# Input chunks ahead of weights, decode steps moved into the mixed stage, splits moved one step forward: one change to a retention-and-two-MLP kernel

## The chip, the cores and the metric

One core of one Trainium2 chip runs the kernel. The time is the device time of one execution in microseconds, the median of three runs: 1015.4 us before the change (1014.79 to 1015.66).

## The reference

Four batches, 8 heads, 768 positions, 64 dimensions per head; everything is float32 on the chip, and the weights come as float64.

```
state = gamma_h * state + k_t (x) v_t ;  y_t = q_t . state / 8      # retention, H=8, S=768
x = y as 3072 tokens x 512
h = (x @ w1) * (x @ w2) @ w3 ;  x = h @ w_out                       # 512 -> 1024 -> 1024 -> 512
h = x @ w_in ;  g = h * sigmoid(1.702 h) ;  out = g @ w_out2        # 512 -> 2048 -> 512
```

## The kernel before, in words

Every product runs on TensorE (PE) as three single-pass matmuls, hi·hi, hi·lo and lo·hi (`mm3`, L231 to L234), so each operand is split: ScalarE (ACT) writes the rounded high part (`split`, L247) and VectorE (DVE) the rest (`residue`, L160).

**Weights.** They arrive as pairs of 32-bit words, 36 tiles of two 512 KB halves ("raw"), fetched through SyncE's (SP's) DMA queue by `fetch` (L107) into `R_BUFS` = 5 buffers. `weight_steps` (L169) turns one tile into floats in eight to ten steps: ACT takes a scaled magnitude (`magnitude`, L126), VectorE clamps, shifts, ors in the low word and the sign; GpSimd (POOL) forms the seven operand blocks of tiles 12 and up (`seven`, L162) and stores them to DRAM. `work(n)` runs n steps: where the code calls it decides where the decode stands on ACT, VectorE and POOL.

**Order.** It is written by hand (`manual_schedule`); each engine runs its instructions in program order, and so does each of the two issuing queues, SP's and POOL's: what stands behind an instruction that waits, waits too.

**Stages.**
1. Attention: 24 chunks of 128 positions, six per batch. `load(c)` (L313, POOL's queue) brings q, k, v of a chunk (128x2048, 1 MB) into one of four buffers; `scores`, `masked`, `updates`, `outputs` work on it; `fill(c, at)` after each of the four runs decode steps and, from c = 6 on, a gate product. The decay factors `dy` of chunk places 1 to 5 are made on POOL (L306) from `cy`, a DMA on SP's queue.
2. Gates: for six blocks of 512 tokens (`ORDER`, n = 0 to 5; n = 0 lies in the attention) and eight tiles t each, `gate_mm` makes 12 matmuls of x·w1 and 12 of x·w2 into two `psm` banks (six buffers) and `gate_out` multiplies them (ACT copy L270, DVE L271); `gate_first` (n < 3) stores pairs from two `h` buffers by SP (L284), `gate_second` builds five sums `g` on VectorE and POOL (L981, L982) and stores them by POOL's queue (L983). The x operand of the next block is reloaded and split beside it (`split_x`). Between the last gates of n = 1 and the first of n = 2 stand the eight rows of w3·w_out (`mix_mm`, 24 matmuls and `work(7)` each). In n = 5 `opening(t)` loads and splits what the next stage starts with.
3. Blend: 21 products (seven per pair of token blocks, each 24 matmuls of 512 columns into two `m` banks) of `h` with the mixed weights. Product n needs `l` loaded by SP (L759, four buffers), its high part by ACT and its low part by VectorE. After each product `ahead` runs four decode steps as long as there are any, and later prepares the next stage.
4. Expand (w_in, sigmoid gate) in four slices of eight quads. `fetch_left` (L503) brings the operand blocks `op<-sp` of 896 KB.
5. Contract (w_out), not touched.

Of the kernel before, what the change touches and what calls it, by code (L numbers as in the profile page):

```python
# [7 lines left out]
F32 = mybir.dt.float32  # L8
# [8 lines left out]
P = 128  # L17
NT = B * S
NCK = S // P
NC = B * NCK  # L20
NP = H // 2
TB = 512
# [20 lines left out]
def tile_kernel(  # L43
# [60 lines left out]
    fetched = used = 0  # L104
    allowed = R_BUFS

    def fetch():  # L107

        nonlocal fetched
        if fetched >= min(used + allowed, 2 * len(tiles)):  # L110
            return
        i, c = divmod(fetched, 2)
        fetched += 1
        src = tiles[i][0][:, c * WC : (c + 1) * WC].bitcast(I32)
        raw = prep.tile([P, WC, 2], I32, tag="r", bufs=R_BUFS, name="raw")
        nc.sync.dma_start(raw, src.rearrange("p (c w) -> p c w", w=2))
        raws.setdefault(i, []).append(raw)

# [40 lines left out]
    def residue(hi, lo, x):  # L159
        nc.vector.tensor_tensor(lo, x, hi.bitcast(F32), ALU.subtract)  # L160

    def seven(i, a1, a2):  # L162
        st = homes["st"].tile([P, 1024], F32, tag="st", bufs=2, name="st")
        four(st, a1, a2)
        store_parts(i, a1, a2, st)

# [121 lines left out]
    class Attention:  # L288
# [122 lines left out]
        def run(self, fill):  # L411

            self.scores(0)
            self.masked(0)
            for c in range(NC):
                if c + 1 < NC:
                    self.scores(c + 1)
                fill(c, 0)
                if c + 1 < NC:
                    self.masked(c + 1)  # L420
                fill(c, 1)
                self.updates(c)
                self.next_state(c)
                if c + 3 < NC:
                    self.load(c + 3)
                if c + 2 in range(2, NCK):
                    self.factors(c + 2)
                fill(c, 2)
                self.outputs(c)
                fill(c, 3)  # L430


# [68 lines left out]
    def fetch_left(n, queue=nc.gpsimd):  # L501
        t = left[n][:, 1].rearrange("p b c -> p (b c)")
        queue.dma_start(t.bitcast(F32), sp[n])  # L503
# [8 lines left out]
    class Expand:  # L512
# [75 lines left out]
        def run(self):  # L588
            self.open = nxt = None
            for n in range(1, NQ):  # L590
                left_tile(n)
                if n < NQ - 1:
                    fetch_left(n)
            self.results = [self.result(j) for j in range(2)]
            split_left(1)
            for s in range(NS):

                for j in range(NQ):

                    def step(at):  # L600
                        nonlocal nxt
                        more = s + 1 < NS
                        if more and (j, at) == (2, 3):
                            nxt = operands(s + 1, self.py)
                            next(nxt)
                        elif more and (j, at) in NEXT:
                            next(nxt)
                        elif s and (j, at) in ((0, 0), (0, 1)):
                            next(nxt)
                        if not more and (j, at) in OPENING:  # L610
                            for run in OPENING[j, at]:
                                run()

                    self.quad(s, j, step)
            for _ in self.fourth():
                pass
# [147 lines left out]
    def split_h(n, a, b, hi):  # L764
        for c, d, t in lo2[n]:
            c0, d0 = max(a, c), min(b, d)
            if c0 < d0:
                lo = t[:, c0 - c : d0 - c]
                split(hi[:, c0 - a : d0 - a], lo, lo.bitcast(F32))
# [3 lines left out]
    def split_wm(n):  # L773
        hi, lo = wm[blends[n][1]]
        split(hi, lo, lo.bitcast(F32))

    def opening(t):
        if t:
            name = blends[t - 1][1]
            wm[name] = wtile("wg")  # L780
            nc.sync.dma_start(
                wm[name][1].bitcast(F32), sm[PART[name]].rearrange("p k c -> p (k c)")
            )
        if t == 1:
            x = spare.tile([P, 7, TB], F32R, tag="ope", name="h0")
            hi2[0] = x[:, NM:]
            load_h(0, 0, NM, x[:, :NM])
        if t == KF - 2:
            for k in (0, 2):
                load_h(1, k, k + 2, prep.tile([P, 2, TB], F32R, tag="r", bufs=R_BUFS, name="h1"))  # L790
        if t in (4, 5, 6):
            split_h(0, t - 4, t - 3, hi2[0][:, t - 4 : t - 3])
        if t in (6, 7):
            split_wm(t - 6)

    def blend(p, ps, todo):
        ws = {
# [19 lines left out]
            nc.gpsimd.dma_start(yd[i][:, e], t)  # L817

        load_turn(2)
        hi2[1], k3 = tile("h", 2), tile("h", 2)[:, 0]  # L820
        load_turn(3)
        held = [p.tile([P, TB], F32, tag="o", bufs=2, name="c")]
        ready = [value()]
        split_h(0, 3, 4, k3.rearrange("p (a t) -> p a t", a=1))
        for n, (i, name) in enumerate(blends):
# [47 lines left out]
    with tc.manual_schedule():  # L873
# [4 lines left out]
        with (  # L878
            tc.tile_pool(name="p0", bufs=1, reuse_waits="tile") as p0,
            tc.tile_pool(name="ps0", bufs=1, space=PSUM, reuse_waits="tile") as ps0,  # L880
        ):
            attention = Attention(p0, ps0)
            nc.sync.dma_start(attention.dv, cv)
            nc.sync.dma_start(attention.mask, cmask)
            fetch()
            attention.load(0)
            fetch()
            attention.load(1)
            nc.sync.dma_start(attention.step[:, :NCK], cstep)
            attention.factors(0)  # L890
            attention.load(2)
            attention.factors(1)
            for n in range(2, R_BUFS):
                fetch()
            gates = 0
            late = []

            def wide():
                return ps0.tile([P, TB], F32, tag="w", bufs=2, name="psg")

            def first_gate():
                nonlocal gates
                late.append((gates, 0, gate_mm(gates, 0, wide)))
                gates += 1

            def fill(c, at):
                work(1)
                while late:
                    gate_first(*late.pop())
                if c in range(13, 21) and at == 1:  # L910
                    d = (c - 13) % 4
                    if c < 17:
                        reload(ORDER[1], d)
                    else:
                        split_x(ORDER[1], d)
                if at == 3 and c >= CPB and gates < min(complete, KF):
                    first_gate()

            work(3)
            attention.run(fill)  # L920
            while gates < KF:
                weight(gates)
                first_gate()
                work(4)
                gate_first(*late.pop())
        with (
# [43 lines left out]
            def gate_second(t, i, ab):  # L970
                nonlocal b12, g
                b = hb[0]
                if t % 2 == 0:
                    b12 = pb.tile([P, TB], F32, tag="b", bufs=2, name="b12")
                    g = pb.tile([P, 5, TB], F32, tag="g", bufs=2, name="g")
                    gate_out(b12, ab)
                    nc.vector.tensor_tensor(g[:, 1], b12, b[:, 0], ALU.subtract)
                    return
                gate_out(g[:, 0], ab)
                nc.vector.tensor_tensor(g[:, 3], g[:, 0], b12, ALU.subtract)  # L980
                nc.gpsimd.tensor_tensor(g[:, 2], g[:, 0], g[:, 1], ALU.subtract)  # L981
                nc.gpsimd.tensor_tensor(g[:, 4], b[:, 1], g[:, 2], ALU.subtract)  # L982
                nc.gpsimd.dma_start(hd[i // 2][:, t // 2, 2:], g)  # L983
                hb.pop(0)

            g = None
            b12 = None
            for n, i in list(enumerate(ORDER))[1:]:
                nxt = ORDER[n + 1] if n + 1 < NB else None
                for t in range(KF):  # L990
# [11 lines left out]
                        split_x(nxt, t - KD)  # L1002
                    if n >= 4 and t > 2:
                        allowed = R_BUFS - 2
                    work((1 if nxt is None else 3) if n > 2 else 8)
                    (gate_second if n > 2 else gate_first)(t, i, ab)
                    while rows < KF and (complete > W3 + rows or (n, t) == (2, KF - 1)):
                        ps = mix_mm(rows)
                        work(7)
                        mix_out(rows, ps)  # L1010
                        rows += 1
                        if rows == KF:
                            stage.close()
                            pb = homes["st"] = stage.enter_context(
                                tc.tile_pool(name="b2", bufs=1, reuse_waits="tile")
                            )
        inner.close()
        homes["st"] = second.enter_context(
            tc.tile_pool(name="wa", bufs=1, side="right", reuse_waits="tile")
# [135 lines left out]
```

## Time and profile before

| | |
|---|---|
| median of the runs | 1015.4 us |
| the profiled execution, its span | 1016.0 us, 1014.2 us |
| PE busy in the span | 971.7 us (96%) |
| VectorE, ScalarE, GpSimd busy | 727.0 (72%), 448.8 (44%), 209.8 us (21%) |
| mean granted TensorE clock | 0.984 of 2.4 GHz |
| DMA | 265 GB/s over the span |

The span runs from the first to the last instruction of the core, the execution's time has 1.8 us more around it. PE is the engine that carries the work, so the time can be read as its busy time plus its gaps. Matmul records have the ends modelled; the clock is a share of full speed, and a stretch at 0.50 runs its matmuls at half pace.

### The profile page before, as it was taken

The page shows a single profiled execution, that of the slowest core. Times are in us where ns is not written, and L with a number is a line of the kernel's source. Part 1 is how long each engine was busy: PE and PEld are TensorE (multiplying, and loading weights), DVE is VectorE, ACT ScalarE, POOL GpSimd, SP SyncE. Part 2 cuts the span into 40 slices and gives each one's busy share as a digit, 9 for nine tenths or more (in the row PEclk, how much of TensorE's full clock was granted, in tenths as well). Part 3 has the DMA queues.
Part 4 walks back from the last instruction along what each step waited for, and adds up shares of the span by engine and source line. Part 5 has one row for each costly group of instructions (what it writes and reads, how often), then busy time and mean ns, then how long its engine had stood idle before and what let it go on. Part 6 is the DMA issues. An engine that isn't in the chain of part 4 may idle for free.

```text
span 1014.2 us, 14850 instructions
## 1 busy us (share of the span) xinstructions
PE 971.7 (96%) x5608; PEld 841.1 (83%) x5608; DVE 727.0 (72%) x954; ACT 448.8 (44%) x793; POOL 209.8 (21%) x254
## 2 busy tenths in 40 slices
PE   4999999999989999899997999999999999999998
PEld 3788778888868888678886999999999888888886
DVE  4767768889998975874883796776868555657662
ACT  4666554442323211455453755454546443445330
POOL 3101000248876764430322000000000000000000
PEclk9899999999989999999997999999999999999999
DMA  8789956569999977998846745546497978767871
GB/s 323 263 279 339 391 203 233 197 219 313 329 319 348 365 253 275 383 321 298 278 161 259 262 205 205 239 178 259 184 332 276 323 241 288 240 188 242 292 243 53
DMA packets 115032, 268.73 MB, mean 265 GB/s; under 512 B 7952, under 2 KB 69520, under 8 KB 105488
## 3 DMA queue, kind: packets, MB, share of 16 engines
q1 hardware_dynamic: 100400, 189.52, 53.4%
q0 software_dynamic: 14560, 78.26, 20.4%
q8 instruction: 44, 0.72, 0.3%
q14 instruction: 28, 0.23, 0.1%
HBM read 165.52 MB, written 102.24 MB: 264 GB/s over the span
## 4 chain that ended last, share of the span: by engine, by line
PE 82%; DVE 5%; DMA 4%; POOL 4%; issue 3%; ACT 2%; POOLq 0%; DVEq 0%; ACTq 0%; SPq 0%
PE m L233 11%; PE m L234 11%; PE m L232 11%; PE psm L233 5%; PE psm L234 5%; PE psm L232 5%; PE a L232 4%; PE a L233 4%; PE a L234 4%; PE e L233 2%; PE e L234 2%; PE e L232 2%; POOL st L157 2%; PE s L331 2%; PE y L381 2%
## 5 line engine op out<-in xcount | busy, mean ns | idle before, releaser
L232 PE MATMUL psm<-xh,wh 128*128 128x512 f32 x320 | 125.7, 393 | 3.6 <-ACT xh L247 3.6
L233 PE MATMUL psm<-xl,wh 128*128 128x512 f32 x320 | 125.6, 392 | 1.0 <-DVE xl L160 1.0
L234 PE MATMUL psm<-xh,wl 128*128 128x512 f32 x320 | 125.2, 391 | 0.0
L232 PE MATMUL m<-h,op 128*128 128x512 f32 x320 | 124.5, 389 | 0.0
L234 PE MATMUL m<-h,op 128*128 128x512 f32 x320 | 124.5, 389 | 0.0
L233 PE MATMUL m<-l,op 128*128 128x512 f32 x304 | 118.3, 389 | 0.0
L654 ACT CAST h<-l 128x2048 fp32r<-128x2048 f32 x38 | 72.3, 1914 | 86.1 <-PE m L234 52.9
L655 DVE TENSOR_TENSOR l<-l,h 128x2048 fp32r<-128x2048 f32 x38 | 85.7, 2287 | 21.9 <-ACT h L654 21.7
L232 PE MATMUL a<-yh,op 128*128 128x384 f32 x256 | 86.5, 338 | 7.8 <-ACT s L523 7.3
L126 ACT ACTIVATE x<-raw 128x512 f32<-128x512 f32 x72 | 46.8, 674 | 92.7 <-DMA raw<-in_wo_dram 49.0
L233 PE MATMUL a<-yl,op 128*128 128x384 f32 x256 | 86.2, 337 | 0.0
L234 PE MATMUL a<-yh,op 128*128 128x384 f32 x256 | 86.1, 336 | 0.0
L660 POOL DMA_DIRECT2D op<-sw x6 | 3.2, 530 | 400.1 <-PE a L234 219.7
L232 PEld LDWEIGHTS psm<-xh,wh 128*128 128x128 f32 x320 | 60.6, 189 | 16.7 <-ACT xh L247 4.0
L233 PEld LDWEIGHTS psm<-xl,wh 128*128 128x128 f32 x320 | 60.6, 189 | 14.2 <-DVE xl L160 1.5
L234 PEld LDWEIGHTS psm<-xh,wl 128*128 128x128 f32 x320 | 60.7, 190 | 12.7
L234 PEld LDWEIGHTS m<-h,op 128*128 128x128 f32 x320 | 60.1, 188 | 12.6
L232 PEld LDWEIGHTS m<-h,op 128*128 128x128 f32 x320 | 60.1, 188 | 12.3
L233 PEld LDWEIGHTS m<-l,op 128*128 128x128 f32 x304 | 57.1, 188 | 11.9
L232 PE MATMUL m<-h,wh 128*128 128x512 f32 x168 | 66.1, 393 | 0.0
L234 PE MATMUL m<-h,wl 128*128 128x512 f32 x168 | 65.9, 392 | 0.0
L160 DVE TENSOR_TENSOR l<-l,h 128x2048 fp32r<-128x2048 f32 x19 | 43.7, 2302 | 30.1 <-ACT h L247 30.1
(148 smaller groups left out, 2234.8 us busy)
## 6 DMA issues: line engine op xcount, KB each, us to landing
gd<-g SPq DMA_DIRECT2D x32, 1344.0 KB, 4.6
qkv<-in_qkv_dram POOLq DMA_DIRECT2D x23, 1024.0 KB, 8.3
l<-gd SPq DMA_DIRECT2D x26, 768.0 KB, 7.2
l<-hd SPq DMA_DIRECT2D x19, 1024.0 KB, 6.9
raw<-in_w_dram SPq DMA_DIRECT2D x32, 512.0 KB, 5.5
hd<-g POOLq DMA_DIRECT2D x12, 1280.0 KB, 8.5
raw<-in_wo_dram SPq DMA_DIRECT2D x24, 512.0 KB, 7.3
l<-gd SPq DMA_DIRECT2D x24, 512.0 KB, 5.1
```

Of the source, the lines that this page charges most:

```text
L126: nc.scalar.activation(x, high, AF.Abs, scale=2.0**16)
L157: nc.gpsimd.tensor_tensor(out, x, y, op)
L160: nc.vector.tensor_tensor(lo, x, hi.bitcast(F32), ALU.subtract)
L232: nc.tensor.matmul(ps, wh, xh, start=start, stop=False, skip_group_check=True)
L233: nc.tensor.matmul(ps, wh, xl, start=False, stop=False, skip_group_check=True)
L234: nc.tensor.matmul(ps, wl, xh, start=False, stop=stop, skip_group_check=True)
L331: nc.tensor.matmul(sc[c][j][:, p, :], qkt[c][r, 1, p, :], qkt[c][r, 0, p, :], start=True, stop=True,)
L381: nc.tensor.matmul(out_y, vs[c][:, 2 * p + j, :], pt[c][:, j, p, :], start=(p < 2), stop=first, skip_group_check=True,)
L654: nc.scalar.copy(hi, x.bitcast(F32))
L655: nc.vector.tensor_tensor(x, x.bitcast(F32), hi.bitcast(F32), ALU.subtract)
L660: queue.dma_start(t.bitcast(F32), sw[PART[name]])
```

## The change

Four parts. **(1)** POOL's queue issues chunks 0 to 3 at once; the first weight fetches are bound by a small VectorE memset to `fill(0, 0)` (two) and `fill(1, 0)` (three); `load` asks for chunk c+4 behind the outputs of chunk c, where it asked for c+3 ahead of them; decode steps start at c = 2, one or two per place. The splits of block n = 1 in chunks 17 to 20 move from place 1 to place 3. **(2)** In n = 2 each gate runs six decode steps, not eight; in n = 5 five of the eight gates run one, not all eight; what is left runs in the blend through `ahead`, four per product. **(3)** In `opening` the splits of `h` stand at t = 3, 4, 5 (4, 5, 6 before) and those of the mixed weights at 4 and 6 (6 and 7); a few buffers are allocated in another order. **(4)** Expand's six first `fetch_left` go through SP's queue, not POOL's.

```
@@ fetch
+    def fetch(held=False):
         raw = prep.tile([P, WC, 2], I32, tag="r", bufs=R_BUFS, name="raw")
+        if held:
+            nc.vector.memset(raw[:, :1], 0)
         nc.sync.dma_start(raw, src.rearrange("p (c w) -> p c w", w=2))
@@ seven
+        st = (st_ready.pop() if st_ready
+              else homes["st"].tile([P, 1024], F32, tag="st", bufs=2, name="st"))
@@ Attention.run
                 self.next_state(c)
-                if c + 3 < NC:
-                    self.load(c + 3)
                 if c + 2 in range(2, NCK):
                     self.factors(c + 2)
                 fill(c, 2)
                 self.outputs(c)
+                if c + 4 < NC:
+                    self.load(c + 4)
                 fill(c, 3)
@@ Expand.run
                 if n < NQ - 1:
-                    fetch_left(n)
+                    fetch_left(n, nc.sync)
@@ opening
-        if t in (4, 5, 6):
-            split_h(0, t - 4, t - 3, hi2[0][:, t - 4 : t - 3])
-        if t in (6, 7):
-            split_wm(t - 6)
+        if t in (3, 4, 5):
+            split_h(0, t - 3, t - 2, hi2[0][:, t - 3 : t - 2])
+        if t in (4, 6):
+            split_wm(t // 2 - 2)
@@ blend
         load_turn(2)
+        held = [p.tile([P, TB], F32, tag="o", bufs=2, name="c")]
         hi2[1], k3 = tile("h", 2), tile("h", 2)[:, 0]
         load_turn(3)
-        held = [p.tile([P, TB], F32, tag="o", bufs=2, name="c")]
@@ attention stage
             nc.sync.dma_start(attention.mask, cmask)
-            fetch()
-            attention.load(0)
-            fetch()
-            attention.load(1)
+            for c in range(4):
+                attention.load(c)
             nc.sync.dma_start(attention.step[:, :NCK], cstep)
             attention.factors(0)
-            attention.load(2)
             attention.factors(1)
-            for n in range(2, R_BUFS):
-                fetch()
...
             def fill(c, at):
-                work(1)
+                if (c, at) in ((0, 0), (1, 0)):
+                    for _ in range(3 if c else 2):
+                        fetch(held=True)
+                if c > 1:
+                    work(1 + (c > CPB and at == 2))
                 while late:
                     gate_first(*late.pop())
-                if c in range(13, 21) and at == 1:
-                    d = (c - 13) % 4
-                    if c < 17:
-                        reload(ORDER[1], d)
-                    else:
-                        split_x(ORDER[1], d)
+                if c in range(13, 17) and at == 1:
+                    reload(ORDER[1], c - 13)
+                if c in range(17, 21) and at == 3:
+                    split_x(ORDER[1], c - 17)
...
-            work(3)
             attention.run(fill)
@@ gates
-                    b12 = pb.tile([P, TB], F32, tag="b", bufs=2, name="b12")
+                    b12 = first_b.pop() if first_b else b12_tile()
...
-                    work((1 if nxt is None else 3) if n > 2 else 8)
+                    work(8 if n == 1 else 6 if n == 2 else 3 if nxt is not None else t < KF - 3)
...
+                            st_ready = [pb.tile([P, 1024], F32, tag="st", bufs=2, name="st")]
+                            first_b = [b12_tile()]
+                            pb.tile([P, 1024], F32, name="gap")
```

How the program's instructions move at three places (an engine's rows in program order; `L..` is the line in each kernel, eight lines later in the changed one).

POOL at the start of the program, before: the first four transfers are chunk 0 in two halves, chunk 1 and chunk 2; the row after the first `dy` product is chunk 3.

```order
L63 MEMSET edge 128x88
L313 DMA qkv<-in_qkv_dram 128x1024 x2
L313 DMA qkv<-in_qkv_dram 128x2048 x2
L306 ISA
L306 TENSOR_TENSOR dy<-dy,step 128x512
L313 DMA qkv<-in_qkv_dram 128x2048
L306 TENSOR_TENSOR dy<-dy,step 128x512
```

The same place in the changed kernel:

```order
L63 MEMSET edge 128x88
L321 DMA qkv<-in_qkv_dram 128x1024 x2
L321 DMA qkv<-in_qkv_dram 128x2048 x3
L314 ISA
L314 TENSOR_TENSOR dy<-dy,step 128x512 x2
L321 DMA qkv<-in_qkv_dram 128x2048
L314 TENSOR_TENSOR dy<-dy,step 128x512
```

Chunk 3 has moved ahead of the `dy` products, and chunk 4 stands behind two of them.

ACT where the blend begins, before: the last three casts of `h` for products 0 and 1, the mixed weights of product 2, then the copies `s` of product 0's two banks and the cast of product 2's `l`.

```order
L247 CAST h<-h_3725 128x512
L247 CAST h<-h_3921 128x1024
L247 CAST h<-h_3923 128x1024
L247 CAST wh<-wl 128x1024
L813 COPY s<-m 128x512 x2
L247 CAST h<-l 128x2048
L247 CAST wh<-wl 128x1024
```

The same place in the changed kernel:

```order
L255 CAST h<-h_3683 128x512
L255 CAST h<-h_3884 128x1024
L255 CAST h<-h_3886 128x1024
L255 CAST wh<-wl 128x1024
L128 ACTIVATE x<-raw 128x512 x2
L821 COPY s<-m 128x512 x2
L255 CAST h<-l 128x2048
L255 CAST wh<-wl 128x1024
```

Two magnitudes of a weight tile now stand ahead of the copies of product 0 and of product 2's cast.

SP at the same place, before: the loads `l` of products 2, 3 and on stand behind the mixed weights, with nothing between them.

```order
L781 DMA wl<-sm_99 128x1024 x2
L759 DMA h_3921<-hd_77 128x2x512
L759 DMA h_3923<-hd_77 128x2x512
L781 DMA wl<-sm_99 128x1024
L759 DMA l<-hd_77 128x4x512 x5
```

In the changed kernel:

```order
L789 DMA wl<-sm_99 128x1024
L767 DMA l<-hd_77 128x4x512 x2
L118 DMA raw<-in_wo_dram 128x1024
L767 DMA l<-hd_77 128x4x512
L118 DMA raw<-in_wo_dram 128x1024
L767 DMA l<-hd_77 128x4x512
L118 DMA raw<-in_wo_dram 128x1024
L767 DMA l<-hd_77 128x4x512
```

Fetches of weight halves now stand between the loads, the first behind product 3's load.

## Rows read from the trace of the kernel before

**Rows 1.** PE's waits, whole span (total us, times, longest)

```profile
PE s L331 <- DMA qkv<-in_qkv_dram: 15.0, 3, 6.8
PE a L232 <- ACT s L523: 7.3, 1, 7.3
PE m L233 <- DVE h L160: 4.0, 1, 4.0
PE psm L232 <- ACT xh L247: 3.6, 1, 3.6
```

**Rows 2.** Timeline 16 to 41 us (start, duration, engine, operation, idle before)

```profile
17.77 0.59 POOL L313 DMA_DIRECT2D qkv<-in_qkv_dram  x1
...
24.86 2.08 PE L331 MATMUL s<-qkv 64*128 64x128 f32 x16 [4.15 <-DMA qkv<-in_qkv_dram]
...
30.50 1.16 PE L331 MATMUL s<-qkv 64*128 64x128 f32 x16
...
33.68 0.48 PE L331 MATMUL s<-qkv 64*128 64x128 f32 x2
...
40.84 0.50 PE L232 MATMUL psg<-xh,wh 128*128 128x512 f32 x1
```

**Rows 3.** Windows (PE, PEld, DVE, ACT, POOL busy; PEclk, DMA share, GB/s)

```profile
0.00:7.00 7.00, 0.24 (x2) 0.25 (x4) 0.00 (x0) 1.28 (x1) 2.62 (x9) 1.00 0.62 194
7.00:13.00 6.00, 1.91 (x18) 1.62 (x18) 2.09 (x5) 3.02 (x10) 0.00 (x0) 1.00 1.01 404
41.00:145.00 104.00, 100.66 (x1248) 81.65 (x1248) 74.74 (x133) 60.74 (x196) 8.80 (x16) 1.00 0.83 303
282.80:289.60 6.80, 5.15 (x11) 3.80 (x12) 6.80 (x11) 3.02 (x6) 4.66 (x8) 0.50 0.94 348
290.00:416.00 126.00, 126.00 (x558) 104.34 (x557) 99.88 (x115) 29.37 (x51) 81.13 (x85) 1.00 0.87 318
```

**Rows 4.** Timeline 268 to 284 us, end of n=2

```profile
269.73 0.67 DVE L271 TENSOR_TENSOR h<-h,psm 128x512 f32<-128x512 f32 x1
...
276.85 0.68 DVE L271 TENSOR_TENSOR h<-h,psm 128x512 f32<-128x512 f32 x1
...
277.55 0.33 SPq L284 DMA_DIRECT2D hd<-h  x1
...
282.77 0.62 ACT L247 CAST xh<-xl 128x512 fp32r<-128x512 f32 x1
```

**Rows 5.** Timeline 415 to 440 us, the start of the blend

```profile
415.70 0.39 PE L232 MATMUL m<-h,wh 128*128 128x512 f32 x1
...
419.74 1.76 POOL L981 TENSOR_TENSOR g<-g 128x512 f32<-128x512 f32 x1 [4.62 <-DVE g L271]
...
423.48 0.57 POOL L983 DMA_DIRECT2D hd<-g  x1 [0.30 <-POOL g L982]
...
429.43 2.08 SPq L759 DMA_DIRECT2D l<-hd  x3
...
435.08 1.91 ACT L247 CAST h<-l 128x2048 fp32r<-128x2048 f32 x1 [1.82 <-DMA l<-hd]
...
439.42 0.50 PE L233 MATMUL m<-l,wh 128*128 128x512 f32 x1 [1.13 <-DVE l L160]
```

**Rows 6.** Waits of SP's queue, 420 to 432 us

```profile
SPq L759 <- DMA hd<-g: 22.3, 1, 22.3
```

**Rows 7.** DMA issues (count, KB each, median us to landing)

```profile
raw<-in_wo_dram SPq DMA_DIRECT2D x24, 512.0 KB, 7.3
op<-sp SPq DMA_DIRECT2D x1, 896.0 KB, 7.3
```

**Rows 8.** Costliest groups, ACT's magnitudes (busy us, mean ns | idle before)

```profile
L126 ACT ACTIVATE x<-raw 128x512 f32<-128x512 f32 x72 | 46.8, 674 | 92.7 <-DMA raw<-in_wo_dram 49.0
```

**Rows 9.** Timeline 538 to 546 us, the start of Expand

```profile
539.05 3.15 POOL L503 DMA_DIRECT2D op<-sp  x6
...
544.86 1.68 ACT L247 CAST op<-op 128x1792 fp32r<-128x1792 f32 x1 [6.63 <-DMA op<-sp]
```

More of the change, by code (lines that the diff above doesn't have):

```diff
@@ L105, in tile_kernel @@
     allowed = R_BUFS
-    def fetch():
+    def fetch(held=False):
         nonlocal fetched
@@ L160, in residue @@
         nc.vector.tensor_tensor(lo, x, hi.bitcast(F32), ALU.subtract)
+    st_ready = []
     def seven(i, a1, a2):
-        st = homes["st"].tile([P, 1024], F32, tag="st", bufs=2, name="st")
+        st = (
+            st_ready.pop()
+            if st_ready
+            else homes["st"].tile([P, 1024], F32, tag="st", bufs=2, name="st")
+        )
         four(st, a1, a2)
@@ L986, in tile_kernel, with b12_tile @@
             g = None
+            def b12_tile():
+                return pb.tile([P, TB], F32, tag="b", bufs=2, name="b12")
             b12 = None
```

## The prediction, made before the change was run

> **What bounds the kernel now.** I read the page's table first: PE is busy for 96% of the span, so a change that leaves PE's matmuls as they are can only move the gaps between them and the stretches at half clock. PE's list of waits therefore came second, to name the gaps [rows 1]: 15.0 us in three waits for chunks, 7.3 us at Expand's start, 4.0 us at the blend's start and 3.6 us at the end of n = 2. The windows came third, because each long gap is followed by a stretch in which the granted clock is 0.50, and that stretch costs as much as the gap: in 282.8 to 289.6 us PE shows 5.15 us of work at half pace, 2.6 us of work at full pace [rows 3]. Then the timelines around the four places say which instruction ended each wait [rows 2, 4, 5, 9]. PE's own order of products is the same in both kernels, so the sum is the sum of what these four places lose or gain.
>
> The profiled execution took 1016.0 us with a span of 1014.2 us; the median of the runs is 0.6 us lower. I add the terms to the 1016.0 us and take the 0.6 us off at the end.
>
> **1. The start.** Before, five weight halves of 0.52 MB compete with the chunks, and chunk 3 is issued only at 17.77 us, since it stands behind a `dy` product that needs the constant `cy`. PE reaches the scores of a next chunk at 24.86 and of another at 30.50, 5.6 us apart while the clock was at half in part of it, and 3.2 us later, at 33.68, the next [rows 2]; the first gate starts at 40.84. In both kernels the first gate stands behind the outputs of chunk 4, and ahead of these stand the scores of chunk 5. So the earliest time is the time by which six chunks of 1.05 MB have come, with at worst all five weight halves among them and about 0.36 MB of constants: 6.3 + 2.6 + 0.36 = 9.3 MB. At 194 GB/s for the first 7 us (1.36 MB) and 404 GB/s behind that [rows 3], the other 7.9 MB take 19.6 us: 26.6 us. About 0.6 us of landing and one more chunk of PE's work, 3.2 us at full pace or 5.6 at half, give 30.4 to 32.8; I take 31.8. The gate starts 9.0 us earlier: **−9.0**. The ends: −13 if the halves are not in the way, −4 if the four loads share the rate so that chunk 0 lands late and the clock stays at half.
>
> The gain is kept only if the rest of the attention isn't later. In 41 to 145 us PE was busy for 100.66 of 104 us, VectorE for 74.74, the DMA share was 0.83 [rows 3]. The decode steps that are not done ahead of c = 2 come back at five per iteration, some three more steps of 0.42 to 0.7 us than before per two chunks; VectorE has 29 us of room in this stretch, so I cost them at nothing. If PE were to wait for VectorE there, the room would have to be gone first. Load c+4 behind the outputs instead of c+3 ahead of them asks at nearly the same time for a chunk that is one later. The splits moved from place 1 to place 3 are four casts on ACT of 0.6 us and stand off the path.
>
> **2. The end of n = 2.** Two `h` products stand 7.12 us apart on VectorE (269.73 and 276.85 [rows 4]), while PE needs 126.0 us for 558 matmuls, 0.226 us each, 5.42 us for a gate's 24 [rows 3]. So VectorE falls behind by 1.7 us per gate. The store of the last pair goes out at 277.55 and frees its `h` buffer only when it has landed; ACT's next `h` copy, and behind it the cast of the next block's operand at 282.77, wait for that [rows 4], and PE waits 3.6 us for the cast [rows 1]. The window from 282.8 holds 1.65 us of idle PE, 0.6 of it the end of that wait, and its half clock costs 2.6 us [rows 3]: 3.6 + 1.05 + 2.6 = 7.2 us. With six steps a gate in place of eight, two steps of 0.42 to 0.68 us go: 7.12 − 1.2 = 5.9 us, 0.5 behind PE per gate. Over eight gates that is 4 us of lag in place of 13, less than the two gates (10.8 us) that the six `psm` buffers can hold besides the one in work, so the store leaves ahead of need. **−7.2**; at worst the wait shrinks and the clock still falls, −2; at best −8.
>
> **3. The blend's start.** Here the steps come back. Before, PE starts product 0 at 415.70 [rows 5], waits 4.0 us for VectorE's low part of `h` [rows 1], and product 3's half starts at 439.42. SP's load for that product stood 22.3 us behind the store `hd<-g` of the last gate pair [rows 6]: POOL's sums at 419.74, the store at 423.48, SP's load at 429.43, ACT's cast 1.91 us at 435.08, then VectorE's part and PE [rows 5]. In the changed kernel VectorE runs three steps fewer in n = 5 and its splits stand one gate earlier, which takes the 4.0 us wait away and brings the store's landing forward by about 3 us, to 426.5. But the program puts a fetch of a weight half on SP behind that same load, and two magnitudes on ACT ahead of product 0's copies and product 2's cast. A fetch of 512 KB takes 7.3 us to land [rows 7], 6 to 8 behind two loads: 432.7 to 434.4. ACT, which serves in order, therefore can't run product 0's copies nor product 2's cast until then. From 433.3 on, a little early in that range: one magnitude of 0.7 us [rows 8], two copies of 0.6 us like the cast at 282.77 [rows 4], the cast of 1.9 and the 2.4 us from its end to PE [rows 5] give 439.5 for product 2. Product 3 follows after 5.4 us of work and 2.6 us lost at half clock, as at the end of n = 2: 447.5, against 439.4 before, about 8 us. VectorE's four decode steps per product (some 2.4 us), its low part (some 2.3), those of the mixed weights and the sums come to over 5.4 us in products 3 to 5, so I let nothing be caught up. **+8.0**; the ends are −3 (the halves land in time and only VectorE's lateness goes) and +13 (the magnitudes of the next tile block once more).
>
> **4. Expand's start.** POOL issues the six `op<-sp` at 539.05, behind its last sums; the first is cast at 544.86 [rows 9], 5.8 us later, and PE starts after a wait of 7.3 us [rows 1]. SP has nothing in the way once the last product is done with the buffer, near 537.6. The landing I take as before: **−1.4**. The one `op<-sp` that went through SP landed in 7.3 us [rows 7] against POOL's 5.8 us, so the lower end is +0.1; the upper is −3. By these two rows SP's queue is the slower one. The Trainium skill, DMA: Bandwidth & Descriptors, section "Issuing engine by pattern", holds the opposite, that queues fed by SyncE or ScalarE are generally faster than GpSimd's; by it the term would be nearer −1.8. The rows here differ in neighbours as well as in queue, so neither is settled by them.
>
> Other edits (allocation order, `held`, the memsets on VectorE, which is idle in the first 7 us [rows 3]) I cost at nothing.
>
> Sum: −9.0 − 7.2 + 8.0 − 1.4 = −9.6. 1016.0 − 9.6 = 1006.4 profiled, 1005.8 as a median.
>
> **Rivals.**
> - *ACT is not blocked in the blend*: the raws land before the copies are due. For it speaks that SP's 22.3 us wait ends as soon as the store lands and the DMA share has room; against, that the raw is issued behind it in any case. Then term 3 is −3 and the sum −20.6: 994.8.
> - *The wait at the end of n = 2 stays*: VectorE still runs behind PE by 0.5 us a gate, and it enters n = 2 late from the mixed rows. Then term 2 is −2: 1011.0.
> - *The attention becomes bound by transfers*, the way to slower. 303 GB/s over 104 us is 31.5 MB [rows 3]; 2.6 MB of weight halves come in besides, since they no longer lie ahead of the first gate. 34.1 MB in the same 104 us want 328 GB/s. If only the span's mean of 265 GB/s were to be had, they would take 129 us, 25 us more, and the sum is +15: 1030. It decides from 9.6 us of extra time on, 34.1 MB in 113.6 us or 300 GB/s. Against it speak 318 and 348 GB/s in stretches that show shares of 0.87 and 0.94, and 404 at the start [rows 3].
> - *The early loads do nothing*, since the rate and not the issue holds the first chunks back: term 1 is −4 and the time 1010.8. It lies within the forecast's own range.
>
> **How the numbers follow.** The forecast 0.66, with a range of its own of 1000 to 1011; ACT not blocked 0.16; the wait at n = 2 stays 0.12; transfer-bound 0.06. Predicted 1005.8. The range of 992.5 to 1012 takes in the first two rivals and leaves out the third and the tails. A measurement of this kernel can tell 0.2%, 2 us, from no change: faster means below 1013.4, slower above 1017.4. Only the transfer-bound case is above; a sum of all the weak ends (−4 − 2 + 8 + 0 = +2, or more at +13) falls around no change. Faster 0.90, same 0.04, slower 0.06.
>
> **What would show it.** Term 1: the first `psg` matmul at 30 to 33 us, and no later waits for `qkv`; wrong if it starts after 37. Term 2: no wait of `psm` for ACT near 270 us, and no half clock there. Term 3: ACT idle before the first `x<-raw` behind the blend's start, waiting for the raw, then PE waiting over 5 us for product 2's `l`; wrong if ACT's copies of product 0 stand within 3 us of its end. Term 4: the six `op<-sp` on SP about 1.4 us after the last product, and the wait at Expand's start near 6 us. The whole is wrong if the attention's windows show a PE busy share below 0.95.

## The result, and the profile after

The changed kernel takes 1029.0 us (1027.6 to 1030.3), the kernel before in the same runs 1015.5 us (1014.8 to 1016.1): 1.0133 times as long, 95% interval 1.0115 to 1.0151. It is slower by 1.3%, where −9.6 us had been forecast. The profiled execution has a span of 1027.1 us, 12.9 more than before, and a mean clock of 0.984 as before. The page's table and PE's longest waits, the answer to [rows 1], come first (total us, times, longest):

```profile
PE 973.2 (95%) x5608; PEld 839.2 (82%) x5608; DVE 717.1 (70%) x959; ACT 449.7 (44%) x793; POOL 212.3 (21%) x248
...
PE psg L242 <- DVE wl L137: 14.0, 8, 3.6
PE m L240 <- ACT h L255: 9.5, 1, 9.5
PE s L339 <- DMA qkv<-in_qkv_dram: 8.3, 3, 5.6
PE m L241 <- DVE l L162: 5.7, 4, 3.0
PE a L240 <- ACT s L531: 5.1, 1, 5.1
```

The waits that the change was priced for are smaller: chunks 8.3 us for 15.0, Expand 5.1 for 7.3, and the 3.6 us of `psm` are gone. Two new ones stand above them: all eight gates of the attention wait for VectorE's `wl` (14.0 us), and one product of the blend waits 9.5 us for ACT.

The table lists what I read off each trace at PE's first matmul of a stage: when the first gate starts, how long the attention takes from there to the end of its last output, then the gates n = 1 to 5, the blend and Expand. Contract takes 228.7 us in every one. The experiments' rows are explained below. Times without an interval are of a single run; in the first experiments the runs of one kernel were spread over 0.5 to 1%, so small things are read from the stages. The stages are those of the one profiled execution, which can lie some us off the median (E2 1027.4, E3 1025.3, E6 1015.8 us).

| kernel | first gate at | attention from there | gates | blend | Expand | time (ratio, interval) |
|---|---|---|---|---|---|---|
| before | 40.8 | 106.1 | 268.8 | 121.7 | 243.8 | 1015.5 |
| changed | 33.3 | 122.2 | 261.3 | 136.1 | 241.0 | 1029.0 (1.0133, 1.0115–1.0151) |
| E1 two steps of lead | 34.3 | 110.8 | 261.2 | 137.0 | 241.9 | 1020.8 (1.0047, 1.0027–1.0067) |
| E2 no step in product 0 | 32.6 | 121.9 | 261.2 | 135.4 | 241.4 | 1032.8 (1.0148, 1.0107–1.0189) |
| E3 before + part 1 | 33.7 | 122.5 | 269.1 | 121.7 | 243.6 | 1028.1 (1.0123, 1.0082–1.0164) |
| E4 before + part 2 | 41.3 | 106.1 | 261.3 | 136.5 | 243.3 | 1023.2 (1.0070, 1.0049–1.0091) |
| E5 before + part 4 | 39.8 | 106.1 | 268.8 | 120.9 | 241.7 | 1012.2 |
| E6 E1 + steps in n = 3, 4 | 36.6 | 110.7 | 266.5 | 125.7 | 241.4 | 1013.1 (0.9969, 0.9951–0.9988) |
| E8 as E6, four steps of lead | 36.0 | 103.0 | 266.1 | 123.9 | 241.0 | 1005.7 (0.9891, 0.9865–0.9916) |
| E9 two steps a product | 33.2 | 121.5 | 261.3 | 136.3 | 243.1 | 1030.3 |
| E10 magnitude later | 33.2 | 122.0 | 261.2 | 129.5 | 241.1 | 1021.9 |
| E11 fetch by POOL | 33.2 | 121.3 | 261.2 | 144.2 | 241.8 | 1036.3 |

The change's own sum: −7.5 + 16.1 − 7.5 + 14.4 − 2.8 = +12.7 us.

**Where 16.1 us went in the attention.** From the first gate to the last output, first in the changed kernel, then before (columns as in [rows 3]):

```profile
33.33:155.51 122.18, 105.98 (x1285) 83.75 (x1281) 81.90 (x148) 66.52 (x211) 9.53 (x16) 0.99 0.78 278
40.84:146.94 106.10, 102.51 (x1285) 83.18 (x1281) 75.01 (x134) 60.90 (x196) 8.80 (x16) 1.00 0.82 300
```

PE idles for 16.2 us in place of 3.6, and is busy for 3.5 us more, about half of that at the half clock behind the last gate's wait (3.4 us from 134.35 on). PE and VectorE of the changed kernel around the third gate (start, duration, operation, idle before):

```profile
61.65 0.40 PE L241 MATMUL psg<-xl,wh 128*128 128x512 f32 x1
63.29 0.50 PE L242 MATMUL psg<-xh,wl 128*128 128x512 f32 x1 [1.25 <-DVE wl L137]
```

```profile
61.89 0.75 DVE L184 TENSOR_SCALAR x<-x 128x512 f32<-128x512 f32 x2
62.56 0.68 DVE L137 TENSOR_TENSOR wl<-x,wh 128x512 fp32r<-128x512 f32 x1
63.16 0.68 DVE L411 TENSOR_TENSOR xb<-y,dy 128x512 f32<-128x512 f32 x1
63.76 0.68 DVE L137 TENSOR_TENSOR wl<-x,wh 128x512 fp32r<-128x512 f32 x1
64.36 0.42 DVE L192 TENSOR_SCALAR x<-x 128x512 int32<-128x512 int32 x1
68.69 0.69 DVE L279 TENSOR_TENSOR h<-h,psg 128x512 f32<-128x512 f32 x1 [3.91 <-PE psg L242]
```

The gate's first two matmuls run; the third needs `wl`, whose first half is ready at 63.2. VectorE makes the second half at 63.76, then one more step, and then it idles 3.9 us for the same gate's product. So the two engines wait for each other in turn, and the third of the stage in which VectorE idles (40.3 of 122.2 us) was not there for PE to use. The counts of steps say why: a gate is issued as soon as its tile's 12th, 22nd, 32nd ... step is done. Decode that starts at c = 2 with four steps a chunk and goes on with five reaches 12 at the last place of c = 4, 22 at that of c = 6, and so on: the very places where gates 0, 1, ... are issued (the code issues gates from c = 4 on; the stage list above, with c = 6, is wrong there). Before, seven steps were done by the end of c = 0 and no gate waited.

**Where 14.4 us went in the blend.** ACT, SP and PE of the changed kernel, the answers to [rows 5, 6]:

```profile
418.39 1.04 ACT L255 CAST wh<-wl 128x1024 fp32r<-128x1024 f32 x1
419.34 0.67 ACT L128 ACTIVATE x<-raw 128x512 f32<-128x512 f32 x1
435.18 0.66 ACT L128 ACTIVATE x<-raw 128x512 f32<-128x512 f32 x1 [15.17 <-DMA raw<-in_wo_dram]
435.74 1.06 ACT L821 COPY s<-m 128x512 f32<-128x512 f32 x2
436.68 1.91 ACT L255 CAST h<-l 128x2048 fp32r<-128x2048 f32 x1
```

```profile
406.10 23.12 SPq L767 DMA_DIRECT2D l<-hd  x2
429.33 0.55 SPq L118 DMA_DIRECT2D raw<-in_wo_dram  x1
```

```profile
438.65 0.80 PE L240 MATMUL m<-h,wh 128*128 128x512 f32 x1 [9.49 <-ACT h L255]
440.97 0.79 PE L241 MATMUL m<-l,wh 128*128 128x512 f32 x1 [1.53 <-DVE l L162]
```

SP holds the fetch behind the loads until 429.33, ACT idles 15.2 us at the second magnitude, and PE waits 9.5 us for the cast behind it, which needed only `l`. The windows show the clock that follows (columns as in [rows 3]):

```profile
431.30:445.00 13.70, 4.82 (x11) 3.45 (x12) 6.37 (x7) 9.22 (x11) 2.17 (x3) 0.50 0.85 325
...
446.00:480.00 34.00, 30.47 (x127) 24.36 (x126) 29.47 (x26) 14.78 (x14) 27.71 (x28) 0.95 0.74 234
```

The half clock lasts 13.7 us, twice the 6.8 us of [rows 3], and costs 4.8 / 2 = 2.4 us. In the second window VectorE is busy for 29.5 of 34 us and POOL for 27.7, and PE is idle for 3.5 us, 3.0 of them in one wait for a low part `l`.

### The profile page after: what moved, and what is told of

It reads as the page before. It is cut to its first block, busy times and chain, and to the rows that moved or that the text cites. A ratio compares the mean times of both kernels' runs of the same rounds, so it can differ in the third digit from the quotient of the medians.

```text
span 1027.1 us, 14851 instructions
## 1 busy us (share of the span) xinstructions
PE 973.2 (95%) x5608; PEld 839.2 (82%) x5608; DVE 717.1 (70%) x959; ACT 449.7 (44%) x793; POOL 212.3 (21%) x248
## 4 chain that ended last, share of the span: by engine, by line
PE 48%; DMA 5%; POOL 4%; issue 3%; DVE 3%; ACT 1%; SPq 0%; POOLq 0%; DVEq 0%; ACTq 0%
PE m L241 9%; PE m L242 9%; PE m L240 9%; PE a L240 4%; PE a L242 4%; PE a L241 4%; PE e L242 2%; PE e L240 2%; PE e L241 2%; DMA hd<-g 2%; POOL st L159 1%; DMA raw<-in_wo_dram 1%; PE c L242 1%; PE c L240 1%; PE c L241 1%
## 5 line engine op out<-in xcount | busy, mean ns | idle before, releaser
L663 DVE TENSOR_TENSOR l<-l,h 128x2048 fp32r<-128x2048 f32 x38 | 85.6, 2286 | 20.5 <-ACT h L662 20.5
L240 PEld LDWEIGHTS psm<-xh,wh 128*128 128x128 f32 x320 | 60.1, 188 | 12.7 <-issue 0.2
L162 DVE TENSOR_TENSOR l<-l,h 128x2048 fp32r<-128x2048 f32 x19 | 46.4, 2441 | 33.2 <-ACT h L255 33.2
```

The costliest lines, as they stand in the source:

```text
L240: nc.tensor.matmul(ps, wh, xh, start=start, stop=False, skip_group_check=True)
L663: nc.vector.tensor_tensor(x, x.bitcast(F32), hi.bitcast(F32), ALU.subtract)
```

## The experiments

**E1: lead in the attention.** Two steps more at chunk 3; the sum of steps and PE's order stay.

```
-                    work(1 + (c > CPB and at == 2))
+                    work(1 + (c > CPB and at == 2) + 2 * ((c, at) == (3, 0)))
```

> The changed kernel with two more decode steps at chunk 3, so that every weight tile is finished one to two places before its gate; the sum of steps and PE's order stay. Theory 1 (the gate stands right behind the low part of its own weight tile, so that PE waits for VectorE at all eight gates): the eight waits of psg for wl, 14.0 us together, and the half clock behind the last of them (1.7 us) go; 1029.0 - 14 to - 16 = 1013 to 1015. Rival (VectorE can't keep up with five steps per chunk, or the weight halves come too late because their fetch was held): the two steps are used up after one or two gates and the waits come back; 1025 to 1029.

Measured: 1020.8 us, 8.2 us under the changed kernel, the attention from the first gate on 110.8 us for 122.2. The waits of `psg` fell from eight to three:

```profile
PE psg L242 <- DVE wl L137: 3.1, 3, 1.7
```

The rival is out: the waits that are left stand at 47, 85 and 124 us, so the lead isn't used up. The theory gave the cause, but two steps of lead take only 11.4 of the 16.1 us, the first gate comes 1.0 us later for them, and the time lies 5.8 us above the range I gave.

**E2: no step in product 0.**

```
             if complete < len(tiles):
-                work(4)
+                work(4 if n else 0)
```

> The changed kernel without decode steps in product 0 of the blend; they run in products 1 to 6. Theory 2 (ACT is held by a magnitude whose weight half was fetched behind product 3's load on SP): product 0's copies and product 2's cast come ahead of the magnitudes, product 2 starts near 432 in place of 438.7, and PE's wait of 9.5 us there shrinks below 3: 1019 to 1023. Rival (VectorE's four steps per product are what is too much): the same work is only moved by one product, the wait moves with it: 1027 to 1031.

Measured: 1032.8 us (its interval holds the changed kernel's ratio), blend 135.4 us for 136.1. Product 2 did start at 427.9, but product 3 then waited 6.9 us for ACT, until 440.4. My theory's number failed; its first half, that ACT is held by the magnitude, held, and moving it by one product moves the wait. The time lies 1.8 us above the rival's range. The run doesn't settle what VectorE's share is.

**E3 and E4: one part alone on the kernel before.** E3 takes all of part 1, E4 one line:

```
-                    work((1 if nxt is None else 3) if n > 2 else 8)
+                    work(8 if n == 1 else 6 if n == 2 else 3 if nxt is not None else t < KF - 3)
```

> The kernel before with part 1 alone (chunks first, decode from chunk 2, loads and splits moved). Theory 1: first gate 7.5 us earlier, then 16.1 us lost at the eight gates: 1015.5 + 8.6 = 1024, attention's end at 155.5. Rival (the loss at the gates comes from elsewhere in the changed kernel): 1008.

> The kernel before with part 2 alone (six steps a gate in n = 2, five in all in n = 5, the rest in the blend). Theory 2: -7.5 at the end of n = 2 and +12 to +15 from the blend: 1020 to 1023. Rival (the blend's loss comes from the other order of the opening's splits and buffers, part 3): -7.5 alone, 1008.

Measured: E3 1028.1 us, with the attention at 122.5 us and every later stage as before; E4 1023.2 us, gates −7.5 and blend +14.8 us. Both stages as the theories had them (E3's median lies 2.8 us above its profiled execution). By stages the parts come to +9.3 us for part 1 up to the attention's end, +7.3 for part 2 and, from E5 below, −2.1 for part 4: +14.5 us, where the whole change has +12.7. Part 3 was not run alone; the 1.8 us between are of the size by which a stage that no edit touches differs from run to run in the table (first gate 39.8 to 41.3).

**E5: part 4 alone.**

```
-                    fetch_left(n)
+                    fetch_left(n, nc.sync)
```

> The kernel before with part 4 alone (op<-sp through SP's queue). Theory: SP issues them when PE is done with the blend's last product, 1.4 us or more ahead of POOL; the wait of 7.3 us at Expand's start becomes 5.1 to 5.4 and the half clock behind it 6.8 us in place of 10.2; from Expand's first product to contract's first 241.0 us in place of 243.8, span 1011.4. Rival (the 2.8 us come from the other allocation of part 3): 243 to 244 us, span 1014.

Measured: Expand 241.7 us, the wait 5.2 us, the half clock behind it 6.8 us for 10.2. So part 4 alone gives 2.1 of the 2.8 us, and the rival (243 to 244) is out. In the changed kernel SP issues right when PE is done:

```profile
552.92 3.49 SPq L511 DMA_DIRECT2D op<-sp  x6
...
558.20 1.68 ACT L255 CAST op<-op 128x1792 fp32r<-128x1792 f32 x1 [4.50 <-DMA op<-sp]
```

5.3 us from issue to cast against POOL's 5.8 [rows 9]. Over all runs the two overlap: 5.2 to 5.6 us in eight runs with SP's queue and 7.0 in E9 (where Expand takes 243.1 us), 5.4 to 5.9 us in the three with POOL's. What all nine runs with SP's queue share is the issue at PE's end, and not 1.4 us or more behind it.

**E6 and E8: both losses undone.** E6 is E1 and four steps a gate in n = 3 and 4, so that about 5 steps reach the blend; E8 gives two steps more of lead (the second pair of lines, which in E6 reads as in E1).

```
-                    work(8 if n == 1 else 6 if n == 2 else 3 if nxt is not None else t < KF - 3)
+                    work(8 if n == 1 else 6 if n == 2 else 4 if nxt is not None else t < KF - 3)
...
-                    work(1 + (c > CPB and at == 2))
+                    work(1 + (c > CPB and at == 2) + 2 * ((c, at) in ((2, 3), (3, 0))))
```

> The changed kernel with two more decode steps at chunk 3 and four steps a gate in n = 3 and 4 in place of three, so that some 5 steps are left for the blend in place of 21. Theory (both losses come from where decode steps stand: right behind their gate in the attention, and in the blend): attention's end near 145, the blend's 136 us from first product to Expand become 118 to 122, Expand 2.8 us shorter; span 1000 to 1004 against 1014.2 before. Rival (VectorE has no room in n = 3 and 4 either): PE waits for VectorE there and the gates end 5 to 15 us later; span above 1008.

> As the run before, but with four more steps, two at the end of chunk 2 and two at chunk 3. Theory (the 3.1 us that the gates still waited for wl with two steps are still too little lead): they go, attention's end 142 to 144, span 997 to 1002. Rival (what remains is VectorE's or the transfers' rate): attention's end stays at 145 or later and the start gets later by the steps' 2.4 us; span as the run before or 2 us more.

Measured: E6 1013.1 us, 0.9969 of before (0.9951 to 0.9988), E8 1005.7 us, 0.9891 (0.9865 to 0.9916): the fastest here, faster than both kernels. No row of PE's waits in E8 names `wl` any more, and its attention from the first gate on takes 103.0 us, 3.1 less than before. Its attention ended at 139.0, ahead of the 142 to 144 that I gave, though the first gate starts 2.7 us later than in the changed kernel; its span of 1003.1 us is 1.1 above the range. E6 missed its span (1014.0 for 1000 to 1004) in three places: its attention ended at 147.3 because its first gate came 2.3 us later than E1's, the gates took 5.3 us more than in E1, and the blend took 125.7. In the gates the rival's numbers came (span above 1008), but not its cause. Its loss stands at the end of n = 4, where VectorE is not short of room but idles for ACT, and ACT for a weight half:

```profile
367.50 0.66 ACT L128 ACTIVATE x<-raw 128x512 f32<-128x512 f32 x1 [14.12 <-DMA raw<-in_wo_dram]
...
368.53 0.62 ACT L255 CAST xh<-xl 128x512 fp32r<-128x512 f32 x1
```

```profile
368.19 0.43 DVE L184 TENSOR_SCALAR x<-x 128x512 f32<-128x512 f32 x1 [7.08 <-ACT x L128]
```

```profile
369.20 0.49 PE L240 MATMUL psm<-xh,wh 128*128 128x512 f32 x1 [1.94 <-ACT xh L255]
```

It is the blend's loss at another place: a magnitude ahead of a cast that PE needs. PE waits 1.9 us for that cast, 1.1 us for the low part behind it, and runs 3.4 us at half clock, some 4.7 of the 5.3 us. Of E8's list, these two rows are the longest in the blend and in the gates:

```profile
PE m L240 <- ACT h L255: 4.1, 1, 4.1
...
PE psm L240 <- ACT xh L255: 1.6, 1, 1.6
```

The 1.6 us are the same magnitude (ACT waits 13.8 us for its half). The 4.1 us are none: ACT has nothing to do before the transfer lands:

```profile
412.16 0.59 ACT L821 COPY s<-m 128x512 f32<-128x512 f32 x1 [1.47 <-PE m L242]
419.68 1.90 ACT L255 CAST h<-l 128x2048 fp32r<-128x2048 f32 x1 [6.93 <-DMA l<-hd]
```

**E9: two steps a product,** to tell ACT's wait from VectorE's load.

```
-                work(4)
+                work(2)
```

> The changed kernel with two decode steps a product in the blend in place of four, so that they take eleven products. Theory A (ACT held by the weight half is one cost, VectorE's four steps a product another): PE still waits 5 to 8 us around product 2 or 3 for ACT, but the waits for l on VectorE (5.7 us, the longest 3.0) and the half clock behind them go; from product 0 to Expand 126 to 130 us, span 1018 to 1022. Rival (ACT's wait is all of it): the blend stays at 134 to 137 us. Rival (VectorE is all of it): 120 to 123 us.

Measured: blend 136.3 us, the first rival's number; my theory A and the rival of VectorE alone are out. The number does not show that ACT's wait is all of it: PE waits for ACT twice (7.0 and 2.9 us) but still 4.7 us for `l` on VectorE, and has two half-clock stretches (10.2 and 6.8 us). ACT waits each time for a weight half:

```profile
437.28 0.66 ACT L128 ACTIVATE x<-raw 128x512 f32<-128x512 f32 x1 [10.36 <-DMA raw<-in_wo_dram]
...
467.16 0.66 ACT L128 ACTIVATE x<-raw 128x512 f32<-128x512 f32 x1 [8.33 <-DMA raw<-in_wo_dram]
```

One wait per weight tile points at the step itself: with `allowed` at three buffers, a tile's second half is asked for in the sign step of the tile before, and its magnitude is emitted in that same step.

**E10 and E11: the magnitude later, and the fetch on another queue.** In E10 the second magnitude of a tile stands ahead of its first clamp, a product later; in E11 only the fetch's queue changes. In both, `hold` is set at the blend's first product and holds from there on.

```
@@ E10, weight_steps
-            if i == 0:
-                magnitude(i)
+            magnitude(i)
...
                 fetch()
                 fetch()
-                magnitude(i + 1)
+                if not hold:
+                    magnitude(i + 1)
```

```
@@ E11, fetch
-        nc.sync.dma_start(raw, src.rearrange("p (c w) -> p c w", w=2))
+        (nc.gpsimd if hold else nc.sync).dma_start(raw, src.rearrange("p (c w) -> p c w", w=2))
```

> The changed kernel; in the blend the second magnitude of a weight tile is no longer emitted in the step that asks for its weight half but only ahead of that tile's first clamp, a product later. All steps, four per product, and all fetches stay. Theory B (the cost is ACT's place in order: a magnitude emitted right behind its own fetch holds ACT for a whole transfer, ahead of the casts that PE needs): product 2 starts at 432 to 434 in place of 438.7, product 3 near 440, the blend takes 122 to 128 us in place of 136.1, span 1014 to 1019. Rival (VectorE's four steps a product): 134 to 137 us, span 1025 to 1028.

> The changed kernel; in the blend the weight halves are fetched through POOL's queue, so that they no longer stand behind the loads l on SP's. Theory A (SP's order is what makes the half late, as the prediction had it): the half lands by 430, product 2 starts before 434, the blend takes 122 to 130 us. Theory B (the half can't be asked for before VectorE's sign step frees its buffer near 426.8, whatever the queue): it lands near 434, product 2 starts at 437 to 438, the blend takes 133 to 136 us, span 1024 to 1027.

Measured: E10's blend takes 129.5 us, so 6.6 of the 14.4 us were ACT's order; product 2 starts at 428.6, earlier than expected, but product 3 waits 4.4 us, and the blend lies 1.5 us above the range I gave. The magnitude still waits 8.3 us for the half, now ahead of product 3's cast:

```profile
424.06 1.92 ACT L256 CAST h<-l 128x2048 fp32r<-128x2048 f32 x1
425.89 1.05 ACT L256 CAST wh<-wl 128x1024 fp32r<-128x1024 f32 x1
435.22 0.66 ACT L129 ACTIVATE x<-raw 128x512 f32<-128x512 f32 x1 [8.29 <-DMA raw<-in_wo_dram]
...
436.73 1.91 ACT L256 CAST h<-l 128x2048 fp32r<-128x2048 f32 x1
```

E11 fits neither theory as a whole. Off SP's queue the half lands 3.8 us earlier, and product 2 starts at 434.8 for 438.7 (product 0 had started 1.0 us earlier), so SP's order is worth some 3 us there; 12.6 of ACT's 15.2 us of waiting stay, as theory B has it, since POOL can't issue before VectorE's sign step:

```profile
426.07 0.53 POOL L119 DMA_DIRECT2D raw<-in_wo_dram  x1 [2.81 <-DVE x L206]
...
431.36 0.66 ACT L129 ACTIVATE x<-raw 128x512 f32<-128x512 f32 x1 [12.56 <-DMA raw<-in_wo_dram]
...
454.50 0.66 ACT L129 ACTIVATE x<-raw 128x512 f32<-128x512 f32 x1 [14.48 <-DMA raw<-in_wo_dram]
```

But the next tile's half then stands behind POOL's own sums and stores (POOL issues it at 446.28), ACT waits 14.5 us again, and the blend takes 144.2 us. A queue with a long wait in it was exchanged for another one.

What the blend's 14.4 us consist of can be read from where each product starts. The table counts from product 0's first matmul and gives the lag behind the kernel before (us):

| kernel | product 2 | product 4 | product 7 | Expand |
|---|---|---|---|---|
| changed | +5.1 | +7.7 | +13.5 | +14.4 |
| E10 magnitude later | −4.5 | +2.7 | +6.8 | +7.7 |
| E6 | +0.4 | +3.9 | +3.9 | +3.9 |
| E8 | −0.3 | +2.1 | +2.1 | +2.1 |

Up to product 4 the changed kernel loses 7.7 us, and E10 gets 5.0 of them back by moving the magnitude. Behind product 4 it loses 6.7 us more, 4.9 of them at product 6, which waits for its low part:

```profile
468.75 0.72 PE L241 MATMUL m<-l,wh 128*128 128x512 f32 x1 [3.03 <-DVE l L162]
```

A half clock of 3.4 us follows. E10 still loses 5.0 us there. E6 and E8, which run out of decode steps by product 1, lose nothing there: this part goes with the decode steps.

## Why the prediction was wrong

- **Step 1, the first gate:** right, though 0.3 us past the 30 to 33 us given: 33.3 us, where 31.8 was taken; −7.5 for −9.0.
- **Step 1, "so I cost them at nothing":** this is the step that failed. It compared sums (29 us of VectorE's time free in 104) and not the order: which step a gate needs, and how many places lie between the two. The answer was zero places, at all eight gates, and the cost 16.1 us. PE did wait for VectorE, though "the room would have to be gone first": a third of VectorE's time was still free. (It also took three more steps per two chunks; the code has two, ten for eight.) The changed order was there to be read in the code: between VectorE's last step for `wl` and its product for the same gate stands a single step. E1 and E8 settle it: with two and four more steps done early, at the same count of work, the stage takes 110.8 and 103.0 us, and it ends 10.4 and 16.5 us earlier, the later first gate included. The prediction's own sign of being wrong, a PE busy share below 0.95 in the attention, came: 106.0 of 122.2 us, 0.87. The transfer-bound rival came near the measured time (1030) by another mechanism, which did not happen: PE's waits for chunks fell. That nearness is luck.
- **Step 2, the end of n = 2:** right, −7.5 for −7.2; E4 has it alone.
- **Step 3, the blend:** the place and the mechanism were right (ACT's magnitude in front of product 0's copies and product 2's cast, product 2 at 438.7 for 439.5), the size was not: +14.4 for +8.0, just past the stated end of +13. The sum that was worked out came true where it ends: product 3 begins at 448.2 for 447.5, and the lag at product 4 is 7.7 us (the 439.4 that it set against 447.5 is the second matmul of product 3, which began at 437.9 before). What failed is "so I let nothing be caught up": it named VectorE's load behind product 3 and priced no further loss, and 6.7 us more were lost there, 3.0 of them in product 6's wait for VectorE. By E10, 6.6 us of the 14.4 are the magnitude's place in ACT's order, and by E11 SP's order makes the half some 3 us late. By E6 and E8 what is lost behind product 4 goes with the decode steps; how it parts between VectorE's own load and POOL's sums beside it was not tried.
- **Step 4, Expand:** right in kind, −2.8 for −1.4: 1.6 us from the earlier issue, 0.5 from the landing, the rest from a shorter half clock. That SP's queue is the slower one, as I read from [rows 7], was not borne out. The Trainium skill, DMA: Bandwidth & Descriptors, section "Issuing engine by pattern", calls SyncE's queue generally faster than GpSimd's; this trace fits it by 0.5 us, 5.3 against 5.8 us, but the runs together (5.2 to 5.6 and once 7.0 us, against 5.4 to 5.9) don't show a difference.

With steps 2 and 4 as forecast and the chunks early, the change was worth −17.8 us in three places; both losses came from where decode steps went. E8's sum against before: −4.8 first gate, −3.1 attention, −2.7 gates, +2.1 blend, −2.8 Expand, −11.3 us.

## What to carry to other kernels

When work that feeds an engine is moved later, don't compare sums of busy time: count for each consumer how many steps lie between the last one it needs and its own place; at zero, two engines with room waited for each other at all eight turns here. Look for an instruction that waits for a transfer asked for in its own step, since it holds everything behind it on its engine until the transfer has landed (14 to 15 us in the changed kernel and E6), and look at what stands ahead in the order of another queue before moving the fetch to it (E11). A half-clock stretch belongs to the price of each long gap: 2.4 us behind the wait of 9.5 us here.

## What the runs showed of the hardware that was not expected

VectorE's and POOL's instructions take longer when they run side by side. In the blend of the changed kernel (VectorE, then POOL):

```profile
438.63 2.29 DVE L162 TENSOR_TENSOR l<-l,h 128x2048 fp32r<-128x2048 f32 x1 [11.84 <-ACT h L255]
...
442.57 1.29 DVE L184 TENSOR_SCALAR x<-x 128x512 f32<-128x512 f32 x2
...
444.67 2.81 DVE L162 TENSOR_TENSOR l<-l,h 128x2048 fp32r<-128x2048 f32 x1
...
464.17 4.52 DVE L162 TENSOR_TENSOR l<-l,h 128x2048 fp32r<-128x2048 f32 x1
```

```profile
444.43 0.91 POOL L159 TENSOR_TENSOR st<-x 128x256 f32<-128x256 f32 x1
445.29 2.79 POOL L159 TENSOR_TENSOR st<-x,st 128x256 f32<-128x256 f32 x1
...
465.25 1.28 POOL L871 TENSOR_TENSOR s<-s 128x512 f32<-128x512 f32 x1
...
467.41 2.42 POOL L871 TENSOR_TENSOR s<-s 128x512 f32<-128x512 f32 x1
```

The same low part takes 2.29 us with POOL idle and 4.52 us beside POOL's sums, and a POOL difference of the same shape 0.91 and 2.79 us, the longer one beside the low part at 444.67 (POOL's durations are rough). Steps with one input lengthen too: the pair of L184 at 442.57, beside POOL's sums at 442.74 and 443.67, takes 1.29 us, the one at 61.89 above 0.75. The rows read as one engine standing until the other is done: POOL's 2.79 us end 0.6 us behind the low part that ends at 447.48, its 2.42 us 1.1 us behind the one that ends at 468.69. The Trainium skill, GPSIMD Engine Reference, section "Specifications", names a cause: GpSimd's SBUF interfaces are shared with VectorE, with contention at VectorE's instructions with two SBUF inputs (or in a two-port mode). The low part has two inputs, and its rows fit that; no run here isolates it. The doubled row makes up 2.2 of the 3.0 us that product 6 is late. In E1 and E4 another row is lengthened, the low part of the mixed weights ahead of it (3.4 us for 1.2), and product 6 waits the same 3.0 us.
